# Forgetting attention and channel mix on one core: batch 1's attention weights turned by TensorE, and small operations moved between engines

## The chip, the cores and the metric

One core of a Trainium2 chip runs the whole program. The time is device microseconds from launch to end; the kernel before took 895.82 us, the median of three runs (895.28 to 895.93). PE is TensorE, DVE is VectorE, ACT is ScalarE, POOL is GpSimd and SP the engine that issues the DMAs.

## The reference, cut to what matters

The input has 8 batches, 8 heads, 576 tokens and 64 columns a head; the channel mix has 512 columns outside and 1024 inside.

```python
scores = scale * np.matmul(q, k.transpose(0, 1, 3, 2))
cum = np.cumsum(np.maximum(s, 0.0), axis=-1)
bias = -(cum[:, :, :, None] - cum[:, :, None, :])
scores = np.where(causal, -1000000000.0, scores + np.minimum(bias, 0.0))
scores = scores - np.max(scores, axis=-1, keepdims=True)
attn = np.exp(scores)
attn = attn / (np.sum(attn, axis=-1, keepdims=True) + 1e-09)
x = np.matmul(attn, v)                    # then heads side by side: (8, 576, 512)
xk = mu_k * x + (1.0 - mu_k) * x_prev     # x_prev: x one token earlier
xr = mu_r * x + (1.0 - mu_r) * x_prev
k = np.maximum(xk @ w_k, 0.0)
out = 1.0 / (1.0 + np.exp(-(xr @ w_r))) * (k * k @ w_v)
```

## The kernel before

Attention goes by visits: a visit is two heads of one batch. Batch 0 has eight shorter visits (query tiles 0 to 2 of four head pairs, then tiles 3 and 4), batches 1 to 7 have four visits each over all queries. A head's 576 queries are five tiles of rows: 64 and four times 128. Operands of the big products are split into a high and a low part, so that two or three passes of PE give float32 accuracy.

Batch 0 goes through `scores`. A product lands in a PSUM bank (tags "s" and "t", two banks each). DVE's masking pass (L859) writes the tile to SBUF (W) and gives the row's extreme, ACT takes the exponentials there and the rows' sums (L877), POOL adds a small constant to the sums (L914), DVE inverts them, and POOL scales the rows (L893). Then `weighted` turns the blocks by PE (L1164) and ACT copies them out of PSUM (L1191).

Batches 1 to 7 go through `split_scores`. The tile stays in its PSUM bank: DVE's masking pass writes back there (L945), ACT takes the exponentials in place (L960), POOL prepares the sums (L969), DVE inverts (L976), and `halves` writes two float16 parts of the scaled weights to SBUF, the first by ACT (L985), the second by DVE (L991). The first 64 and the last 128 queries share a bank ("the corner"): for these a DVE operation joins two minima (L1023) and two POOL operations add and copy sums (L1033, L1043). `turn_by_dma` then turns the parts by transposing DMAs into T (four a head), and `sum_values` multiplies them by V's two parts.

V is scaled by POOL (L710) to use float16's range and split by ACT (L715) and POOL (L717). K's high part is a cast on ACT (L777), its low part a difference on POOL (L781), its other copy a cast on POOL (L787); Q's are L792 and L796.

The channel mix goes by 18 chunks of 256 tokens, each of which needs all heads of its tokens. One chunk is 96 products with w_k (L1380), 24 with w_r (L1422) and 48 with w_v (L1447).

Nothing runs in the order of the code. Every instruction is recorded as a task with a cost and a due time, and `Plan` lays them out with a model of the engines; each engine then runs its list in that order, waiting where an operand or a buffer is not there. So the cost written beside an operation (the numbers at the end of `pool(...)` or `act(...)`) sets only the order.

## Time and profile before

| | |
|---|---|
| median of 3 runs | 895.82 us |
| the profiled execution | 894.85 us, its span 893.0 us |
| busy: PE, DVE, ACT, POOL | 831.0, 657.1, 671.5, 453.3 us |
| mean granted clock of PE | 0.96 of full speed |
| PE matmuls | 5094 |

The span is the time from the first to the last instruction of the profiled execution. PE's busy time is not PE at its peak, since matmuls are pipelined and their ends are modelled. In the page's 40 slices PE's granted clock is 0.9 or more in all but five, which lie among the sixth to the eleventh slice, about 112 to 246 us.

### The profile page before, as it was taken

To read this page: it belongs to the slowest core of one execution; us is meant where nothing else is said; L and a number is where in the kernel's file an instruction comes from. 1 tells how busy PE (TensorE), PEld (TensorE's weight loads), DVE (VectorE), ACT (ScalarE), POOL (GpSimd) and SP (SyncE) were. 2 spreads that over 40 slices of the span, in tenths; PEclk is the share of its full clock that TensorE was granted. 3 is DMA by queue.
4 is the path that set the end of the run, shared out by engine and by line. 5 is a ranking of instruction groups with operands and counts; after the bars stand their busy time and mean duration, and the time that the engine had idled before them with its cause. 6 is when DMAs were issued, how large, how long until landed. Compare 5 with 4: busy or idle time off the path is not lost. (4 is left out here: it accounts for less than half of the span.)

```text
span 893.0 us, 16962 instructions
## 1 busy us (share of the span) xinstructions
PE 831.0 (93%) x5094; PEld 664.0 (74%) x5094; DVE 657.1 (74%) x1879; ACT 671.5 (75%) x1703; POOL 453.3 (51%) x755
## 2 busy tenths in 40 slices
PE   9989968866899998999999999999999999999998
PEld 7778747643668777777777877777777778788986
DVE  8989867656788788777887787878787778555431
ACT  6999887656888788788887786878797887545331
POOL 6898884556365555556465465465556552000000
PEclk9999978975799999999999999999999999999999
DMA  8776385687679977796677868679787756401100
GB/s 244 238 230 195 94 182 130 146 160 164 140 161 188 164 169 157 168 187 144 150 182 163 186 156 173 134 153 185 159 163 163 178 102 129 97 22 36 49 25 23
DMA packets 248828, 131.48 MB, mean 147 GB/s; under 512 B 208864, under 2 KB 222176, under 8 KB 248736
## 3 DMA queue, kind: packets, MB, share of 16 engines
q1 hardware_dynamic: 248736, 130.40, 65.0%
q8 instruction: 40, 0.66, 0.3%
q14 instruction: 52, 0.43, 0.2%
HBM read 61.47 MB, written 19.33 MB: 90 GB/s over the span
## 5 line engine op out<-in xcount | busy, mean ns | idle before, releaser
L1380 PE MATMUL m<-xh,w_k 128*128 128x256 f32 x976 | 199.5, 292 | 11.7 <-DVE kl L1409 9.0
L1447 PE MATMUL m<-w_v,kh 128*128 128x512 f32 x528 | 176.8, 400 | 2.5 <-ACT g L1434 2.4
L1380 PEld LDWEIGHTS m<-xh,w_k 128*128 128x128 f32 x976 | 160.7, 194 | 22.6 <-DVE kl L1409 12.2
L1380 PE MATMUL m<-xl,w_k 128*128 128x256 f32 x488 | 140.4, 288 | 0.0
L1447 PEld LDWEIGHTS m<-w_v,kh 128*128 128x128 f32 x528 | 99.0, 189 | 25.7 <-ACT g L1434 2.8
L1447 PE MATMUL m<-w_v,kl 128*128 128x512 f32 x264 | 105.8, 401 | 0.0
L991 DVE SCALAR_TENSOR_TENSOR W<-s,rinv,W 128x64 f16<-128x64 f32 (+2 forms) x168 | 76.6, 458 | 31.8 <-ACT W L985 31.0
L781 POOL TENSOR_TENSOR KH<-raw,KH 64x576 fp32r<-64x576 f32 x64 | 90.7, 1417 | 15.6 <-ACT KH L777 12.1
L1319 ACT ACTIVATE xp<-x,mu 128x256 f32<-128x256 f32 (+3 forms) x184 | 78.3, 426 | 24.8 <-DMA x<-x_d 12.6
L969 POOL TENSOR_SCALAR rinv<-sums 128x1 f32<-128x1 f32 (+1 forms) x224 | 43.1, 192 | 106.2 <-ACT s L960 61.0
L1380 PEld LDWEIGHTS m<-xl,w_k 128*128 128x128 f32 x488 | 94.5, 194 | 2.4 <-issue 0.9
L1422 PE MATMUL m<-w_r,xh 128*128 128x512 f32 x264 | 93.1, 404 | 2.6 <-DVE kl L1409 2.6
L933 PE MATMUL s<-KH,G 128*64 128x64 f32 (+2 forms) x224 | 66.5, 305 | 29.6 <-DVE W L991 29.1
L1326 DVE SCALAR_TENSOR_TENSOR xp<-x,mu,xp 128x256 f32<-128x256 f32 (+3 forms) x184 | 76.5, 416 | 21.1 <-ACT xp L1319 18.3
L796 POOL TENSOR_TENSOR QL<-raw,G 64x576 fp32r<-64x576 f32 (+1 forms) x64 | 85.4, 1334 | 11.6 <-ACT G L792 8.9
L1103 PE MATMUL po<-T,V 128*64 128x512 f16 (+5 forms) x672 | 88.8, 351 | 0.8 <-DMA T<-W 0.8
L985 ACT ACTIVATE W<-s,rinv 128x64 f16<-128x64 f32 (+2 forms) x168 | 76.3, 458 | 16.7 <-DVE rinv L976 7.2
L960 ACT ACTIVATE s<-s,nm 128x64 f32<-128x64 f32 (+2 forms) x168 | 71.4, 425 | 18.6 <-DVE nm L945 14.8
L991 DVE SCALAR_TENSOR_TENSOR W<-t,rinv,W 128x320 f16<-128x320 f32 (+1 forms) x112 | 71.9, 645 | 10.8 <-ACT W L985 10.6
L960 ACT ACTIVATE t<-t,nm 128x320 f32<-128x320 f32 (+1 forms) x112 | 65.0, 581 | 18.7 <-DVE nm L1023 13.7
L933 PEld LDWEIGHTS s<-KH,G 128*128 128x128 f32 (+1 forms) x224 | 41.2, 184 | 50.9 <-DVE W L991 40.7
L945 DVE CUSTOM_DVE_ANT_0 t<-t,lower 128x320 f32<-128x320 f32 (+1 forms) x112 | 66.9, 599 | 10.1 <-PE t L933 9.5
(185 smaller groups left out, 2039.9 us busy)
## 6 DMA issues: line engine op xcount, KB each, us to landing
raw<-in_q SPq DMA_DIRECT2D x112, 144.0 KB
vn<-in_v SPq DMA_DIRECT2D x28, 384.0 KB
raw<-in_k SPq DMA_DIRECT2D x32, 288.0 KB
out<-g SPq DMA_DIRECT2D x36, 256.0 KB
x_d<-xT SPq DMA_DIRECT2D x28, 288.5 KB
x<-x_d SPq DMA_DIRECT2D x11, 514.0 KB
w_k<-in_moe_w_k SPq DMA_DIRECT2D x8, 512.0 KB
w_v<-in_moe_w_v SPq DMA_DIRECT2D x8, 512.0 KB
```

Of the source, the lines that this page charges most:

```text
L781: lambda own=own, other=other, K=K: nc.gpsimd.tensor_tensor(out=K.get()[other], in0=k.get()[own], in1=f32(K.get()[own]), op=ALU.subtract),
L796: lambda x=x, QQ=QQ, QL=QL: nc.gpsimd.tensor_tensor(out=QL.get()[0:64, 0:nq], in0=x.get()[0:64], in1=f32(QQ.get()[0:64]), op=ALU.subtract,),
L933: lambda x=x, G=G, K=K, r=r: nc.tensor.matmul(ps.get()[:m, :n], G.get()[:r, q : q + m], K.get()[:r, k0 : k0 + n], start=x == 0, stop=x == 1,),
L960: lambda: nc.scalar.activation(ps.get()[:, :n], ps.get()[:, :n], AF.Exp, bias=nm.get()[:, i : i + 1], scale=-1.0, accum_out=sums.get()[:, ...
L985: lambda: nc.scalar.activation(part(0), ps.get()[:, :n], AF.Copy, scale=rinv.get()[:, i : i + 1]),
L991: lambda: nc.vector.scalar_tensor_tensor(out=part(1), in0=ps.get()[:, :n], scalar=rinv.get()[:, i : i + 1], in1=part(0), op0=ALU.mult, op1 ...
L1103: nc.tensor.matmul(po.get()[64 * j : 64 * j + 64, start:n], V.get()[:, x, kb, j], at(y, kb, j), start=i == 0, stop=False, tile_position=(0 ...
L1319: lambda z=z: nc.scalar.activation(to(*z), source(1, *z), AF.Copy, scale=mu.ap[:, which, c + z[0] : c + z[0] + 1]),
L1326: lambda z=z: nc.vector.scalar_tensor_tensor(out=to(*z), in0=source(0, *z), scalar=mu1.ap[:, which, c + z[0] : c + z[0] + 1], in1=to(*z), ...
L1380: lambda u=u, f=f, c=c, n=n, w=w, x=x: nc.tensor.matmul(ps.get()[:, u * CT : (u + 1) * CT], weight["k", c, f // 4].get()[:, w, f % 4 * P : ...
L1422: lambda c=c, n=n, x=x, w=w: nc.tensor.matmul(ps.get(), x.get()[:, c, ts], weight["r", c, 0].get()[:, w], start=c == 0 and n == 0, stop=c ...
L1447: lambda f=f, n=n, x=x, w=w: nc.tensor.matmul(ps.get(), x.get()[:, f, ts], weight["v", f, 0].get()[:, w], start=f == 0 and n == 0, stop=f ...
```

## The change

Batch 1 leaves `split_scores` and `turn_by_dma`. It goes through `scores` as batch 0 does, with the sums scaled for float16, and `turn_by_pe` turns the blocks: 14 transposes a head into "t" banks, each block copied by ACT to T as the high float16 part, and the rest written by DVE as the low part, in the layout that `sum_values` reads. Three memsets a head on POOL clear what no block fills. V of batch 1 is laid out after the first head's turn.

For batches 2 to 7 the corner minimum is a DVE reduction, with ACT copying the lower rows; the corner sums and the sums' preparation move from POOL to ACT; K's high part moves from ACT to POOL. V's scaling has a second operation (times 1.0) in all batches. A column of zeros and ones (`upper_rows`) is made once.

```diff
             lambda: nc.gpsimd.tensor_scalar(
-                out=whole(), in0=whole(), scalar1=scales.get()[:, 1:2], scalar2=None, op0=ALU.mult,
+                out=whole(), in0=whole(), scalar1=scales.get()[:, 1:2], scalar2=1.0,
+                op0=ALU.mult, op1=ALU.mult,
             ),
...
+            if b < BY_DMA:
+                act(
+                    lambda own=own, K=K: nc.scalar.copy(K.get()[own], k.get()[own]),
...
+            else:
+                pool(
+                    lambda own=own, K=K: nc.gpsimd.tensor_copy(K.get()[own], k.get()[own]),
+                    [(k, j)], [(K, j)], nk, 150, 0.8333, (2 * j, 2 * j),
+                )
...
         def inverses(i, e, o):
-            pool(
-                lambda: nc.gpsimd.tensor_scalar(
-                    out=rinv.get()[:, i:e], in0=sums.get()[:, o : o + e - i],
-                    scalar1=1.0e-9, scalar2=1.0 / HALF, op0=ALU.add, op1=ALU.mult,
-                ),
...
+            act(
+                lambda: nc.scalar.activation(
+                    rinv.get()[:, i:e], sums.get()[:, o : o + e - i], AF.Copy,
+                    bias=1.0e-9 / HALF, scale=1.0 / HALF,
+                ),
...
             dve(
-                lambda: nc.vector.tensor_scalar(
-                    out=upper(nm, LAST, c + 1), in0=upper(nm, LAST, c + 1),
-                    scalar1=upper(nm, LAST, c), scalar2=upper(nm, c, c + 1),
-                    op0=ALU.min, op1=ALU.min,
-                ),
...
+                lambda: nc.vector.tensor_reduce(
+                    out=upper(nm, LAST + 2, c + 3),
+                    in_=upper(nm, LAST, c + 1).unsqueeze(1).broadcast_to([64, 2, 2]),
+                    axis=mybir.AxisListType.X, op=ALU.min,
+                ),
...
+            act(
+                lambda: nc.scalar.copy(nm.get()[0:64, LAST + 2 : c + 3], nm.get()[0:64, LAST : c + 1]),
...
+            for x, y in ((LAST, c), (c, LAST)):
+                act(
+                    lambda x=x, y=y: nc.scalar.activation(
+                        sums.get()[:, x + 2 : x + 3], sums.get()[:, y : y + 1], AF.Identity,
+                        scale=upper_rows.ap, bias=sums.get()[:, x : x + 1],
+                    ),
...
+    def turn_by_pe(pt):
+
+        T, n = sbuf([P, ROWS * (S - 64)], "T", TURNED, F16), S - 64
...
+            pool(
+                lambda rows=rows, w=w, a=a, step=step: nc.gpsimd.memset(
+                    blocks(w, a, step).bitcast(F32)[rows], 0.0
+                ),
...
+        def turn(ps, place, t, k0, m):
+            pe(
+                lambda: nc.tensor.transpose(
+                    ps.get()[0:m, place : place + P], pt[t].get()[:, k0 : k0 + m], ident.ap
+                ),
...
+        def halves(src, first, second, ps, n, keys, to=0):
+            act(lambda: nc.scalar.copy(first(), src()), [ps], [(T, (0, x)) for x in keys], n)
+            dve(
+                lambda: nc.vector.tensor_tensor(
+                    out=second(), in0=src(), in1=first(), op=ALU.subtract
+                ),
...
+        for kb in range(LAST - 1):
+            ps = bank(1, "t", 2)
+            block(ps, 0, kb)
+        block(ps, 2 * P, LAST - 1)
...
-            Ts.append(turn_by_dma(pt[0]))
+            Ts.append(turn_by_dma(pt[0]) if by_dma(n) else turn_by_pe(pt))
...
-            if n >= PLAIN:
+            if by_dma(n):
                 pt = split_scores(QKs[n][j], parts16[j], None if j else Vs[n][1])
```

POOL's list in batch 1, before: from one scaling of V (vn) to the inverse sums of the next head's tiles (rinv; KL, KH and QL are K's and Q's parts).

```order
L710 TENSOR_SCALAR vn_93<-vn_93,scales_1492 128x768
L694 TENSOR_SCALAR scales_1255<-scales_1255 128x1
L787 CAST KL_533<-raw_284 64x576
L1033 TENSOR_TENSOR sums_135<-sums_135 64x2
L781 TENSOR_TENSOR KH_529<-raw_284,KH_529 64x576
L1043 COPY sums_135<-sums_135 64x2
L717 TENSOR_TENSOR V_1536<-vn_93,V_1536 128x768
L969 TENSOR_SCALAR rinv_239<-sums_135 128x2
```

The same engine in batch 1 of the changed kernel, again from a scaling of V.

```order
L716 TENSOR_SCALAR vn_94<-vn_94,scales_1835 128x768
L809 TENSOR_TENSOR QL_131<-raw_372,G_708 64x576
L724 TENSOR_TENSOR V_1869<-vn_94,V_1869 128x768
L927 TENSOR_SCALAR rinv_250<-sums_136 128x5
L809 TENSOR_TENSOR QL_110<-raw_451,G_425 64x576
L906 TENSOR_SCALAR W_184<-W_184,rinv_250 128x192
L906 TENSOR_SCALAR W_184<-W_184,rinv_250 128x320
L906 TENSOR_SCALAR W_184<-W_184,rinv_250 128x448
L906 TENSOR_SCALAR W_184<-W_184,rinv_250 64x64
L906 TENSOR_SCALAR W_184<-W_184,rinv_250 128x576
L800 CAST KL_549<-raw_92 64x576
```

The corner's two operations and the single inverse sums are gone from POOL; one inverse sum of five columns stands for a whole head, and five scalings of the rows of W follow it.

ACT's list at a corner in batch 2, before: the exponentials of the bank "t" and of the corner's bank "s" (sums_135), and the first halves of the same head (W_1310).

```order
L960 ACTIVATE t_275,sums_135<-t_275,nm_184 128x512
L960 ACTIVATE s_149,sums_135<-s_149,nm_184 128x64
L960 ACTIVATE t_272,sums_157<-t_272,nm_226 128x320
L715 CAST V_1536<-vn_93 128x768
L1319 ACTIVATE xp_297<-x_155,mu 128x192 x2
L960 ACTIVATE s_151,sums_135<-s_151,nm_184 128x192
L985 ACTIVATE W_1310<-s_149,rinv_239 128x64
```

The same engine at a corner in the changed kernel (sums_136, W_2245).

```order
L1046 COPY nm_185<-nm_185 64x2
L999 ACTIVATE W_2420<-s_153,rinv_305 128x448
L974 ACTIVATE t_321,sums_136<-t_321,nm_185 128x512
L974 ACTIVATE s_151,sums_136<-s_151,nm_185 128x64
L1415 ACTIVATE xp_309<-x_157,mu 128x256
L1054 ACTIVATE sums_136<-sums_136,upper_rows 128x1 x2
L1415 ACTIVATE xp_309<-x_157,mu 128x256
L983 ACTIVATE rinv_250<-sums_136 128x2
L999 ACTIVATE W_2245<-s_151,rinv_250 128x64
```

Four small operations of the corner, which stood on POOL and DVE, now stand between ACT's own, with one operation of other work between the exponentials, the sums and the inverse sums.

## Rows read from the trace of the kernel before

**Rows 1.** Busy time by stretch: us, then each engine; clock, DMA share.
```profile
0.00:112.00 112.00, 105.26 (x650) 87.26 (x651) 98.40 (x256) 98.53 (x269) 93.33 (x153) 0.98 0.68 199
112.00:212.00 100.00, 77.85 (x412) 55.88 (x410) 65.64 (x203) 69.51 (x179) 58.63 (x98) 0.79 0.73 157
...
250.00:800.00 550.00, 529.54 (x3352) 421.24 (x3352) 426.61 (x1268) 441.60 (x1119) 281.05 (x473) 1.00 0.73 155
```

**Rows 2.** Timeline of ACT: start, us, engine, line, operation.
```profile
111.83 0.37 ACT L1261 COPY xT<-po 64x256 f32<-64x256 f32 x1
...
212.12 0.69 ACT L1149 ACTIVATE xT<-po,scales 128x512 f32<-128x512 f32 x1
```

**Rows 3.** Busy time by stretch, two slices of 10 us in batch 1.
```profile
190.00:200.00 10.00, 4.11 (x13) 3.00 (x13) 6.21 (x22) 6.78 (x18) 5.98 (x12) 0.50 0.56 118
...
220.00:230.00 10.00, 5.25 (x18) 2.76 (x19) 6.48 (x22) 8.79 (x25) 8.10 (x12) 0.50 0.95 190
```

**Rows 4.** Waits, 112 to 212 us: total us, times, longest.
```profile
PE s L933 <- DVE W L991: 11.7, 6, 5.6
```

**Rows 5.** Timeline of all engines, 193.8 to 201.7 us; idle time before in brackets.
```profile
193.92 2.23 POOL L710 TENSOR_SCALAR vn<-vn,scales 128x768 f32<-128x768 f32 x1
...
196.18 0.83 ACT L715 CAST V<-vn 128x768 f16<-128x768 f32 x1 [1.88 <-POOL vn L710]
...
199.31 0.19 POOL L1033 TENSOR_TENSOR sums<-sums 64x2 f32<-64x2 f32 x1 [0.58 <-ACT s L960]
...
201.54 0.53 PE L933 MATMUL s<-KH,G 128*128 128x192 f32 x1 [5.63 <-DVE W L991]
```

**Rows 6.** Groups by line, POOL: count, busy us, mean ns, idle before.
```profile
L710 POOL TENSOR_SCALAR vn<-vn,scales 128x768 f32<-128x768 f32 x28 | 62.3, 2224 | 6.2 <-DVE scales L692 3.5 <-POOL KH L781 0.9 <-DVE rinv L976 0.2
...
L969 POOL TENSOR_SCALAR rinv<-sums 128x1 f32<-128x1 f32 (+1 forms) x224 | 43.1, 192 | 106.2 <-ACT s L960 61.0 <-ACT t L960 29.6 <-PE s L933 1.5
...
L787 POOL CAST KL<-raw 64x576 fp32r<-64x576 f32 x64 | 42.2, 660 | 42.2 <-PE s L933 31.9 <-issue 6.4 <-PE t L933 1.3
...
L1043 POOL COPY sums<-sums 64x2 f32<-64x2 f32 x56 | 10.0, 178 | 2.2
...
L455 POOL MEMSET T<- 64x64 f32 x4 | 0.6, 238 | 0.1
```

**Rows 7.** Single lines: count, shortest/median/longest ns, first and last start, forms.
```profile
L893 POOL TENSOR_SCALAR W<-W,rinv x40: 311/534/757, 11.2 to 103.8; 128x192 f32<-128x192 f32 x8, 128x320 f32<-128x320 f32 x8, 64x64 f32<-64x64 f32 x8, 128x448 f32<-128x448 f32 x8
...
L877 ACT ACTIVATE W<-W,nm x40: 333/561/788, 7.4 to 98.2; 64x64 f32<-64x64 f32 x8, 128x192 f32<-128x192 f32 x8, 128x320 f32<-128x320 f32 x8, 128x448 f32<-128x448 f32 x8
L877 ACT ACTIVATION_READ_ACCUMULATOR W<-W,nm x40: 184/190/248, 7.6 to 98.9; 128x1 f32 x32, 64x1 f32 x8
...
L1164 PE MATMUL t<-ident,W x112: 270/273/421, 12.5 to 108.3; 128*128 128x128 f32 x80, 128*64 128x128 f32 x32
```

**Rows 8.** Groups by line, ACT and DVE.
```profile
L985 ACT ACTIVATE W<-s,rinv 128x64 f16<-128x64 f32 (+2 forms) x168 | 76.3, 458 | 16.7 <-DVE rinv L976 7.2 <-issue 4.9 <-ACT W L985 1.4
...
L960 ACT ACTIVATE s<-s,nm 128x64 f32<-128x64 f32 (+2 forms) x168 | 71.4, 425 | 18.6 <-DVE nm L945 14.8 <-DVE rinv L976 2.2 <-DVE scales L687 0.3
L985 ACT ACTIVATE W<-t,rinv 128x320 f16<-128x320 f32 (+1 forms) x112 | 67.6, 611 | 3.4 <-ACT t L960 1.5 <-DVE rinv L976 0.5 <-ACT V L715 0.4
...
L960 ACT ACTIVATE t<-t,nm 128x320 f32<-128x320 f32 (+1 forms) x112 | 65.0, 581 | 18.7 <-DVE nm L1023 13.7 <-DVE nm L945 4.3
...
L777 ACT CAST KH<-raw 64x576 fp32r<-64x576 f32 x64 | 42.9, 670 | 2.4 <-PE s L933 1.6
...
L1023 DVE TENSOR_SCALAR nm<-nm 64x2 f32<-64x2 f32 x56 | 28.8, 514 | 2.0
...
L1191 ACT COPY T<-t 128x256 f32<-128x256 f32 (+2 forms) x40 | 14.5, 375 | 2.1 <-PE t L1164 1.9
```

**Rows 9.** Timeline of PE, 12 to 13 us: four transposes in a row.
```profile
12.52 0.60 PE L1164 MATMUL t<-ident,W 128*64 128x128 f32 x4
```

**Rows 10.** Waits, 250 to 800 us: total us, times, longest.
```profile
POOL sums L1033 <- ACT s L960: 53.9, 28, 4.9
```

More of the change, by code (lines that the diff above doesn't have):

```diff
@@ L434, in forgetting_attention_then_channel_mix @@
     HALF = 2.0**15
+    upper_rows = fixed(const.tile([P, 1], F32, name="upper_rows"))
+    for i in range(2):
+        pool(
+            lambda i=i: nc.gpsimd.memset(upper_rows.ap[64 * i : 64 * i + 64], 1.0 * i),
+            [], [(upper_rows, i)], 1, 100,
+        )
     LAST = NQ - 1
@@ L1027, in last_and_first @@
                 ),
[L1028 removed]
+                [(nm, LAST), (nm, c)], [(nm, "u")], 4, quarters=(2, 2),
             )
[L1030 to L1041 removed]
@@ L1074, in turn_by_dma, with parts, blocks, block @@
             )
-        return T
+        def parts(y, kb):
+            return [(T, t) for t in range(max(kb, 1), NQ)]
+        return T, parts
+    def turn_by_pe(pt):
+        T, n = sbuf([P, ROWS * (S - 64)], "T", TURNED, F16), S - 64
+        def blocks(w, a, step, k=LAST - 1):
+            x = T.get().rearrange("p (x q) -> p x q", q=w)
+            return x[:, a : a + step * (k - 1) + 1 : step]
+        for rows, w, a, step, key in (
+            (slice(64, P), 64, 9, 10, 0),
+            (slice(0, 64), 64, 24, 18, 1),
+            (slice(64, P), P, 12, 9, 2),
+        ):
+            pool(
+                lambda rows=rows, w=w, a=a, step=step: nc.gpsimd.memset(
+                    blocks(w, a, step).bitcast(F32)[rows], 0.0
+                ),
+                [], [(T, ("z", key))], w * 3 // 2, 150,
+            )
+        def turn(ps, place, t, k0, m):
[3 more added lines that the diff above has]
+                ),
+                [(pt[t], i) for i in range(3)] + [ident], [ps], P, m, 2 / 2.4,
+            )
+        def halves(src, first, second, ps, n, keys, to=0):
[4 more added lines that the diff above has]
+                ),
+                [ps] + [(T, (0, x)) for x in keys], [(T, (1, x)) for x in keys], n,
+                quarters=(0, to),
+            )
+        def block(ps, place, kb):
+            k = LAST - kb
+            for t in range(kb + 1, NQ):
+                turn(ps, place + P * (t - kb - 1), t, kb * P, P)
+            halves(
+                lambda: ps.get()[:, place : place + P * k].rearrange("p (x q) -> p x q", q=P),
+                lambda: blocks(P, n // P * kb + kb, 1, k),
+                lambda: blocks(P, 9 * kb + 8, 5, k),
+                ps, P * k, [kb],
+            )
+        ps = bank(1, "t", 2)
+        for t in range(1, NQ):
+            turn(ps, P * (t - 1), t, t * P, 64)
+        halves(
+            lambda ps=ps: ps.get()[0:64].rearrange("p (x q) -> p x q", q=64)[:, 0:8:7],
+            lambda: blocks(64, 8 * MIXED + 6, 1, 2)[0:64],
+            lambda: blocks(64, 8 * MIXED + 6, 1, 2)[64:P],
+            ps, P, ["m"], 2,
+        )
+        halves(
+            lambda ps=ps: ps.get()[0:64].rearrange("p (x q) -> p x q", q=64)[:, 1:6:2],
+            lambda: blocks(64, 9, 10)[0:64],
+            lambda: blocks(64, 25, 18)[0:64],
+            ps, 192, ["c"],
+        )
+        for kb in range(LAST - 1):
+            ps = bank(1, "t", 2)
+            block(ps, 0, kb)
+        block(ps, 2 * P, LAST - 1)
+        def parts(y, kb):
+            if kb == LAST:
+                return [(T, (y, "m")) for y in range(2)]
+            found = [(T, (y, kb))]
+            if kb:
+                found += [(T, (y, "c"))] + [(T, ("z", x)) for x in ((1, 2) if y else (0,))]
+            return found
+        return T, parts
@@ L1083, in at @@
         def at(y, kb, j):
-            x = Ts[j].get()
+            x = Ts[j][0].get()
             if not y:
@@ L1110, in both @@
                     )
-            ts = range(max(kb, 1), NQ)
             before = [(po, ("sum", 0))] if i else []
             pe(
-                both, [(V, x)] + [(T, t) for T in Ts for t in ts] + before,
+                both, [(V, x)] + Ts[0][1](y, kb) + Ts[1][1](y, kb) + before,
                 [(po, ("sum", i))] + ([po] if not i else []), n - start, 64, 1.05 / 2.4,
@@ L1143, in sum_values @@
             after = [(po, ("sum", len(todo) + x))] + ([po] if x else [])
-            pe(ends, [(V, x)] + [(T, LAST) for T in Ts] + before, after, 64, 64, 1.05 / 2.4, k)
-            pe(firsts, [(V, x)] + [(T, LAST) for T in Ts], [rest], 64, 64, 1.05 / 2.4, k)
+            pe(ends, [(V, x)] + Ts[0][1](0, LAST) + Ts[1][1](0, LAST) + before, after, 64, 64, 1.05 / 2.4, k)
+            pe(firsts, [(V, x)] + Ts[0][1](0, LAST) + Ts[1][1](0, LAST), [rest], 64, 64, 1.05 / 2.4, k)
         for q0, w, ps in ((0, 64, rest), (64, n, po)):
```

56 lines of the change are left out of this document (26 added, 30 removed).

## The prediction

> **What bounds the kernel now.** I read the busy time by stretch first [rows 1]. The kernel has three different stretches, and the change bears on two of them. Up to 112 us batch 0 is prepared and the weights are turned into two float32 parts: ACT is busy 98.53 of 112 us (0.88) and POOL 93.33 (0.83). From 250 to 800 us PE is busy 529.54 of 550 us (0.96) at the full clock, so that stretch is PE's, with 20.5 us idle. In between, from 112 to 212 us, nothing is full: PE has 77.85 us of work at a mean granted clock of 0.79, ACT 69.51, DVE 65.64, POOL 58.63.
>
> Why nothing is full there is read from the ends of the visits [rows 2]. The last copy of batch 0 into xT starts at 111.83 us and the last one of batch 1 at 212.12 us, so batch 1's four visits (eight heads) take 100.3 us. A chunk of the channel mix has 256 tokens and a batch 576: two chunks lie in batch 0, the third needs batch 1. So PE has two chunks to put between batch 1's heads and then only attention. In the two slices shown [rows 3] PE is busy 4.11 and 5.25 of 10 us, at a clock of 0.50, which is the 1.2 GHz level. It got there after idling. What PE waits for is named next [rows 4]: the matmul of the scores (L933) waits 11.7 us in this stretch for DVE's second half of the weights (L991), that is, for its PSUM bank. Under `split_scores` a bank holds a tile from the product until both halves of the weights are written, and there are two banks of each tag.
>
> One such wait shows the chain [rows 5]. POOL scales V in one operation of 2.23 us from 193.92; ACT's V cast behind it waits 1.88 us, the exponentials wait behind that cast, POOL's sums follow at 199.31, the bank is free only when all that is over, and PE starts again at 201.54 after 5.63 us idle. So the stretch is bound by a chain over four engines with a bank held all along.
>
> What the stretch saves reaches the end: after it PE is 0.96 busy until 800 us [rows 1], and what follows is channel mix alone. PE's work itself shrinks nowhere.
>
> **Batch 1 turned by PE (eight heads).** The products go through `scores`: DVE moves a tile into SBUF in its one masking pass and the bank is free. The chain that held the bank is gone; what is late next is whichever engine has most to do.
> POOL, per head, from its rows [rows 6]. Gone: four inverse sums, 43.1 us over 56 heads, 0.77; the two small corner operations, 2 x 0.18 = 0.36; V's scaling in the new form. The new form is the two-operation tensor_scalar of L893 [rows 7]: 0.757 us for its longest tile, of 576 columns, and 0.311 for the shortest, of 64, so 0.92 for 768 against 2.224, per head half of it, 0.65. Together 1.78. Added: five normalisations of 0.534, 2.67; one inverse sum 0.19; three small memsets of T and one of a column, 0.15 each by L455's 0.6 us for four, 0.5. Together 3.36. Net +1.58, times eight +12.6: 58.6 becomes 71.2 us.
> ACT, per head [rows 7, 8]. Gone: L960, (71.4 + 65.0)/56 = 2.44, and L985, (76.3 + 67.6)/56 = 2.57. Added: five exponentials on SBUF at 0.561, 2.81, and six copies of together 1600 columns at L1191's rate (14.5 us for eight heads of 1280 columns in batch 0), 2.27. The five sum readouts are there before and after. Net +0.07: ACT stays at 70 us.
> DVE loses three of four reciprocals and the corner minimum, and gets six subtractions over 1600 columns for five multiply-subtractions over 1536; I cost this at nothing, hidden by POOL, which has more to do than DVE's 65.64.
> PE gets 14 transposes a head. Four in a row take 0.60 us [rows 9]; less the 0.27 of a single one [rows 7], which the other three follow into the array, that is 0.11 each: 112 are 12.3 us at the full clock. PE's 77.85 us at 0.79 are 61.5 at the full clock, so 73.8 in all.
> SP loses the 32 transposing DMAs of batch 1, so its queue and the loads behind them only get earlier; I take nothing for it.
>
> How long is the stretch then? No engine runs at 1.0. Batch 0 takes the same path, and there POOL reached 0.83 and ACT 0.88 [rows 1]. POOL: 71.2/0.83 = 86 us. ACT: 70/0.88 = 80 us. PE at the full clock 74, at 0.79 93 us. The ends are 80 and 93; I take POOL's 86, because it is the longest of those that the likeliest clock leaves. The gain is 100.3 - 86 = 14.3 us.
>
> The GPSIMD Engine Reference of the Trainium skill (section 4.1, Engine selection) has one-input operations on GpSimd at about line rate. L710's 2.224 us for 768 columns is not that, while L893's 0.757 for 576 is near it. By the page alone the second operation would bring nothing: POOL would be left with 76.4 us and the stretch with 92, a gain of 8 instead of 14.
>
> **Batches 2 to 7 (48 heads).** V's scaling: 1.3 us a visit off POOL; by [rows 5] it was ahead of the sums. The corner minimum: 0.514 us [rows 8] falls to that of another small DVE operation, at best 0.3 saved a head. Both lie beside PE, which is 0.96 busy. POOL no longer stands waiting for ACT's sums (53.9 us before L1033 alone, [rows 10]), so K's and Q's parts behind those waits get earlier. K's high parts cost POOL 0.66 each (as the cast L787, [rows 6]), 48 x 0.66 = 32 us, against 48 x 1.78 = 85 us taken off: hidden in a POOL that is half idle.
> ACT is the other side. It loses 0.67 (L777, [rows 8]) and gets seven small operations a head: the lower rows' minimum, two corner sums, four inverse sums. No such operation is in the trace. From below: 0.19, the readout of one column; from above: 0.333, the shortest exponential, of 64 columns [rows 7]. I take 0.25, nearer to the 64-column one less its columns. Seven are 1.75, less 0.67 is 1.08 a head, 52 us over 48 heads: ACT goes from 441.6 to 493 of 550 us, from 0.80 to 0.90. That is still under PE's 0.96. A small operation that waits for ACT's own sum holds up what is queued behind it on ACT: other heads' halves, and the casts that channel mix waits for. Against the shorter chain I take -2 us for this stretch, between -10 (half of PE's 20.5 idle) and the slower rival below.
>
> **The sum.** 894.85 - 14.3 - 2 = 878.5 us for the profiled execution, which stood 0.97 below the median of the runs; I predict 878.
>
> **Rivals.**
> *The clock stays low.* If PE is granted 0.79 as now, its own work in the stretch, 73.8 at the full clock, takes 93 us, and PE is the bound: gain 7, time 887. For it: PE idles between attention pieces now and the clock is at half [rows 3]. Against it: with the banks free PE's work comes denser, and in batch 0, with the same transposes, the clock is 0.98 [rows 1]. [...]
> *More is gained.* POOL's order lets it run as full as ACT in batch 0 (0.88) and the shorter chain fills half of PE's later idle time: 100.3 - 80 = 20 and 10 more, time 865. For it: POOL waits for ACT only once a head then. Against it: PE's last 3 to 4% are small gaps at many lines.
> *Slower: ACT becomes the bound of batches 2 to 7.* With seven operations at 0.333 it gets 2.33 - 0.67 = 1.66 a head, 80 us: 522 of 550. If each of six of them also waits 0.19 for the sum's readout ahead of it, 55 us more, 577: more than the stretch has, and the stretch grows by 27 against 14 won: 908. It decides from ACT's 564 us on (550 and the 14 won). For it: ACT is in order and each corner sum needs two results of ACT itself. Against it: the order puts other work between (a halves operation or the mixes of the channel mix), and ACT reached 0.88 beside PE in batch 0.
> *No change.* PE's idle time only moves to the wait for batch 2's heads behind 212 us: within 2 us of now, 895.
>
> **Chances.** The forecast (80 to 93 us for the stretch, 872 to 887) 0.56; low clock 0.20; more gained 0.14; slower 0.07; no change 0.03. The forecast, the low clock and the larger gain are all faster: 0.90 by over 0.2% (1.8 us, about what a measurement of this kernel can tell from no change), 0.03 within, 0.07 slower. The range 862 to 892 takes in the forecast's, the low clock's and most of the larger gain and leaves out the slower case.
>
> **What would show it.** Right: batch 1's last xT copy at about 198 us; no wait of over 3 us of the scores' matmul for a PSUM bank before it; V's scaling at 0.9 us; POOL above 0.8 and the clock above 0.9 in the stretch; ACT about 0.9 busy from there to 800. Wrong: that copy at 207 us or later with a clock near 0.8 (the second case); ACT at 0.95 and PE waiting for ACT's casts in batches 2 to 7 (the slower case); V's scaling still above 2 us, which takes 6 us off the gain.

## The result and the profile after

The changed kernel takes 851.41 us (median of 4 runs, 850.28 to 854.97), the kernel before 895.67 beside it (895.28 to 895.93): a ratio of 0.951, with a 95% interval of 0.948 to 0.954. That is 44 us less, where 18 were forecast, and below the range's lower end. The profiled execution took 850.28 us with a span of 848.5; the other stood at 894.85 and 893.0.

The marks that answer to [rows 2], in the timeline of ACT after: the last copy of batch 0, the last of batch 1, and the last visit's.

```profile
105.64 0.37 ACT L1357 COPY xT<-po 64x256 f32<-64x256 f32 x1
...
189.91 0.69 ACT L1245 ACTIVATE xT<-po,scales 128x512 f32<-128x512 f32 x1 [0.68 <-PE po L1218]
...
734.60 0.69 ACT L1245 ACTIVATE xT<-po,scales 128x512 f32<-128x512 f32 x1 [0.82 <-PE po L1218]
```

The ends of these copies cut the span into four stretches. Busy time by stretch, first the kernel after (the answer to [rows 1]; columns as there), then the kernel before with the same cuts.

```profile
0.00:106.00 106.00, 100.54 (x624) 84.50 (x625) 90.94 (x238) 95.59 (x263) 88.33 (x152) 0.97 0.62 197
106.00:190.60 84.60, 82.63 (x555) 63.30 (x553) 60.65 (x203) 66.73 (x190) 70.08 (x120) 1.00 0.37 106
...
190.60:735.30 544.70, 528.89 (x3396) 425.05 (x3396) 434.68 (x1348) 476.23 (x1468) 250.89 (x279) 0.97 0.78 167
735.30:848.50 113.20, 109.46 (x644) 95.85 (x642) 47.74 (x83) 41.60 (x81) 0.00 (x0) 1.00 0.10 32
```

```profile
112.20:212.80 100.60, 78.45 (x413) 56.53 (x412) 65.44 (x203) 70.03 (x180) 58.91 (x101) 0.78 0.73 157
212.80:779.90 567.10, 537.71 (x3391) 424.30 (x3391) 445.08 (x1338) 460.89 (x1176) 300.86 (x503) 0.98 0.75 158
779.90:893.00 113.10, 109.35 (x644) 95.73 (x642) 47.95 (x83) 41.81 (x82) 0.00 (x0) 1.00 0.10 33
```

| stretch | before | after | gain | forecast gain |
|---|---|---|---|---|
| batch 0 | 112.2 | 106.0 | 6.2 | 0 |
| batch 1 | 100.6 | 84.6 | 16.0 | 14.3 |
| batches 2 to 7 | 567.1 | 544.7 | 22.4 | 2 |
| after the last visit | 113.1 | 113.2 | -0.1 | 0 |

So the step on which most of the argument was spent came out, and half of the gain lies where nearly none was expected. Between the two ends of batches 2 to 7 PE has the same matmuls (3391 and 3396 records, 2046 of the channel mix in both), yet its busy time is 8.8 us shorter and its idle time goes from 29.4 to 15.8. The waits that got shorter there are seen in this pair, of batches 2 to 7 alone, before and after (us in total, times, longest): PE for an "s" bank that DVE frees, ACT's cast of V for POOL's scaling, and ACT for the corner minimum. The second has no row in the answer after any more.

```profile
PE s L933 <- DVE W L991: 17.3, 17, 4.1
...
ACT V L715 <- POOL vn L710: 11.6, 15, 1.8
...
ACT t L960 <- DVE nm L1023: 10.1, 18, 2.0
```

```profile
PE s L947 <- DVE W L1005: 6.9, 10, 1.6
...
ACT t L974 <- DVE nm L1038: 1.9, 5, 0.6
```

### The profile page after: what moved, and what is told of

Read it like the earlier page. It is cut to its first block, busy times and chain, and to the rows that moved or that the text cites. A ratio compares the mean times of both kernels' runs of the same rounds, so it can differ in the third digit from the quotient of the medians.

```text
span 848.5 us, 17084 instructions
## 1 busy us (share of the span) xinstructions
PE 821.5 (97%) x5214; PEld 668.7 (79%) x5214; DVE 634.0 (75%) x1871; ACT 680.1 (80%) x1999; POOL 409.3 (48%) x549
## 4 chain that ended last, share of the span: by engine, by line
PE 83%; DVE 7%; ACT 7%; issue 2%; DMA 2%; SPq 0%; POOL 0%; ACTq 0%; DVEq 0%; POOLq 0%
PE m L1543 22%; PE m L1476 15%; PE m L1518 10%; PE po L1200 8%; PE s L947 5%; PE t L947 4%; PE po L1346 2%; PE s L857 2%; PE t L1543 2%; PE t L1476 2%; PE s L1476 2%; PE t L1116 2%; PE t L1260 1%; PE s L846 1%; PE s L835 1%
## 5 line engine op out<-in xcount | busy, mean ns | idle before, releaser
L1415 ACT ACTIVATE xp<-x,mu 128x256 f32<-128x256 f32 (+3 forms) x184 | 78.7, 428 | 22.4 <-DMA x<-x_d 13.4
L790 POOL CAST KH<-raw 64x576 fp32r<-64x576 f32 x48 | 31.7, 660 | 119.2 <-PE s L947 106.0
L1200 PE MATMUL po<-T,V 128*64 128x512 f16 (+5 forms) x672 | 79.7, 339 | 1.0 <-DMA T<-W 1.0
L1005 DVE SCALAR_TENSOR_TENSOR W<-s,rinv,W 128x192 f16<-128x192 f32 (+2 forms) x144 | 65.3, 456 | 12.1 <-ACT W L999 9.8
L999 ACT ACTIVATE W<-s,rinv 128x192 f16<-128x192 f32 (+2 forms) x144 | 66.2, 463 | 4.0 <-DVE rinv L990 3.1
L1005 DVE SCALAR_TENSOR_TENSOR W<-t,rinv,W 128x320 f16<-128x320 f32 (+1 forms) x96 | 61.8, 645 | 10.1 <-ACT W L999 9.5
L974 ACT ACTIVATE s<-s,nm 128x64 f32<-128x64 f32 (+2 forms) x144 | 62.1, 431 | 8.2 <-DVE nm L959 7.4
L959 DVE CUSTOM_DVE_ANT_0 t<-t,lower 128x320 f32<-128x320 f32 (+1 forms) x96 | 57.5, 601 | 11.3 <-PE t L947 10.4
L999 ACT ACTIVATE W<-t,rinv 128x320 f16<-128x320 f32 (+1 forms) x96 | 58.7, 618 | 2.0 <-DVE rinv L990 1.8
L947 PE MATMUL s<-KH,G 128*128 128x192 f32 (+2 forms) x192 | 52.8, 289 | 7.1 <-DVE W L1005 6.9
L1518 PEld LDWEIGHTS m<-w_r,xh 128*128 128x128 f32 x264 | 49.2, 189 | 12.0 <-DVE kl L1505 0.9
```

Source lines behind the costliest of these rows:

```text
L947: lambda x=x, G=G, K=K, r=r: nc.tensor.matmul(ps.get()[:m, :n], G.get()[:r, q : q + m], K.get()[:r, k0 : k0 + n], start=x == 0, stop=x == 1,),
L974: lambda: nc.scalar.activation(ps.get()[:, :n], ps.get()[:, :n], AF.Exp, bias=nm.get()[:, i + o : i + o + 1], scale=-1.0, accum_out=sums.g ...
L999: lambda: nc.scalar.activation(part(0), ps.get()[:, :n], AF.Copy, scale=rinv.get()[:, i : i + 1]),
L1005: lambda: nc.vector.scalar_tensor_tensor(out=part(1), in0=ps.get()[:, :n], scalar=rinv.get()[:, i : i + 1], in1=part(0), op0=ALU.mult, op1 ...
L1200: nc.tensor.matmul(po.get()[64 * j : 64 * j + 64, start:n], V.get()[:, x, kb, j], at(y, kb, j), start=i == 0, stop=False, tile_position=(0 ...
L1415: lambda z=z: nc.scalar.activation(to(*z), source(1, *z), AF.Copy, scale=mu.ap[:, which, c + z[0] : c + z[0] + 1]),
```

## The experiments

Times are medians; the ratio is to the kernel before, on the same chip, with its 95% interval. "Stretches" are batch 0, batch 1, batches 2 to 7 and the rest, in us, cut here at the starts of the last copies, which puts them up to 0.7 us off a cut at the ends.

### The parts of the change, each alone

The first question was which part the 22 us of batches 2 to 7 belong to: the theory was V's scaling, rivals the corner or a mere reordering of the list.

**Turn alone (turn_only).** The kernel after, with the other edits undone.

> The kernel before with batch 1 turned by PE and nothing else of the change. Theory A (each edit pays in its own batches; the 22 us that batches 2 to 7 lost come from the edits to their small operations): batch 1's stretch is 16 us shorter and batches 2 to 7 keep their 567 us, so 874 to 880 us. Rival B (once batch 1 is dense, batches 2 to 7 run denser too, whatever their small operations): 850 to 862, with batches 2 to 7 at about 545 us.

**All but the turn (no_turn).** The same number decides who casts K's high part, so batch 1's casts go to POOL as well.

```diff
-    BY_DMA = 2
+    BY_DMA = 1
```

> The changed kernel, but batch 1 goes by split_scores and transposing DMAs like batches 2 to 7, with all other edits. Theory A: batches 2 to 7 take about 545 us, batch 1's stretch 100 us less its share of the same edits (22/6 = 4 us): 866 to 873 us. Rival B: close to before, 888 to 895.

**V's second operation alone (v_only).** On the kernel before:

```diff
-scalar2=None, op0=ALU.mult,
+scalar2=1.0, op0=ALU.mult, op1=ALU.mult,
```

> The kernel before with V's scaling in two operations alone: POOL gets 1.3 us a visit back. Theory A1 (the inverse sums on POOL were the chain, and V's scaling stood ahead of them): 8 to 12 us faster, 884 to 888. Rival A2 (what counts is that ACT needs no other engine for the sums): 0 to 3 us faster, 893 to 896.

**The corner alone (corner_only).** On the kernel before, the reduction on DVE, and all sums on ACT, as in the change's diff.

> The kernel before with the corner minimum as a DVE reduction and all sums on ACT, in batches 1 to 7; V's scaling in one operation, K's high part on ACT. ACT gets seven small operations a head more, 1.8 us. Theory A2: 15 to 20 us faster, 876 to 881, in batches 2 to 7 above all. Theory A1: 4 to 8 us faster, 888 to 892, since V's scaling still holds POOL and ACT. Rival C (ACT has too much without moving K's part): slower than before.

**A cost number alone (order_only), and K's high part (k_only).** Only the written cost of one cast, which the change also alters; then K's part on POOL from batch 2 on, with the same number.

```diff
-                [(k, j)], [(KB, 0)], nk, 244, 0.8333, (2 * j, 0),
+                [(k, j)], [(KB, 0)], nk, 150, 0.8333, (2 * j, 0),
```

> The kernel before with one number of the change alone, the cost written beside K's third copy on POOL (244 becomes 150), which sets the order of the lists and no instruction. Theory A: within 0.5% of before, 890 to 899, so that the gains of 15 us of single edits are theirs. Rival O (any new order is worth about 15 us against the one of before): 875 to 885.

> The kernel before with K's high part cast by POOL in batches 2 to 7 and no other edit (with the cost 150 of that copy's neighbour). ACT loses 0.67 us a head, POOL gets 0.66. Theory A (POOL's waits for the sums hold K's parts and the next head): 0 to 8 us slower, 895 to 903. Rival D (ACT's time is what counts in these batches): 8 to 15 us faster, 880 to 887.

**K's high part back on ACT (after_k_act)**, in the kernel after, with the 244 of its neighbour; and **half of batch 1 turned by PE (turn_half)**, its first two visits, the last two by DMA as the batches behind it, a test of whether the change of path between batch 1 and batch 2 costs something:

```diff
-        return visits[n][0] >= BY_DMA
+        return n >= PLAIN + NP // 2
```

> The changed kernel with K's high part back on ACT (and the cost 244 of its neighbour). ACT has seven more operations a head and keeps the cast. Theory D2 (the small operations on ACT pay only together with K's part off ACT, since ACT was at 505 of 566 us with the first alone): 8 to 15 us slower than the changed kernel, 859 to 866. Rival: the same as the changed kernel, 850 to 855.

> The changed kernel with the first two visits of batch 1 turned by PE and the last two by transposing DMAs, all other edits kept. Theory H (the hole at the change from one path to the other, 27 us at a clock of 0.62 behind batch 1, is the price of the turn: with no turn at all the first visit of batch 2 took 19.8 us): the change of path falls where chunks of batch 0 are left for PE, so 843 to 848. Rival: between the changed kernel and the one without a turn, 852 to 858.

| kernel | us | ratio | stretches |
|---|---|---|---|
| before | 895.67 | | 111.8, 100.3, 567.1, 113.8 |
| turn_only | 879.06 | 0.983 (0.979 to 0.987) | 105.9, 82.1, 573.1, 114.1 |
| v_only | 879.24 | 0.984 (0.980 to 0.987) | 111.0, 94.1, 557.4, 113.9 |
| corner_only | 876.37 | 0.982 (0.977 to 0.986) | 110.8, 92.4, 566.0, 105.0 |
| k_only | 893.71 | 0.999 (0.997 to 1.001) | 112.1, 97.3, 567.5, 114.2 |
| order_only | 897.29 | 1.003 (1.000 to 1.005) | 112.9, 103.1, 567.7, 114.0 |
| no_turn | 858.62 | 0.960 (0.957 to 0.963) | 114.2, 94.5, 535.4, 113.1 |
| turn_half | 859.51 | 0.961 (0.959 to 0.964) | 107.9, 99.5, 533.5, 115.7 |
| after | 851.41 | 0.951 (0.948 to 0.954) | 105.6, 84.3, 544.7, 113.9 |
| after_k_act | 849.35 | 0.951 (0.947 to 0.955) | 106.1, 85.6, 540.0, 116.0 |

What follows. Everything but the turn gives 37.1 us, and that is nearly the sum of its parts alone (V 16.4, corner 19.3, K 2.0: 37.7). K's move is worth nothing that can be told, in either direction. The turn alone gives 16.6, but on top of the rest only 7. In this set batches 2 to 7 get much shorter only where V's edit and the corner's stand together (534 to 545 us); alone they leave 557 and 566. But a list also moves pieces of the channel mix from one stretch to another, so a length means little without the work in it: PE has 3378 to 3396 matmuls in this stretch in all these runs but corner_only, which has 3459 there and 70 fewer behind the last visit. The hypothesis about the change of path fell: with the change inside batch 1 the first visit of batch 2 is short, 20.5 us, as in no_turn (19.8; 27.8 before, 27.7 after), but batch 1 takes 99.5, and the total is no_turn's.

Of the expectations, turn_only's and order_only's came. corner_only's total came, but not its place: it has 7.9 us in batch 1 and 8.8 behind the last visit, and hardly any in batches 2 to 7. v_only came 5 us and no_turn 7 us below what was expected, turn_half 12 above, k_only between its two ranges, and after_k_act just below its rival's.

Busy time by stretch of turn_only (batch 1, batches 2 to 7) and of no_turn (the same), columns as above:

```profile
106.30:188.70 82.40, 80.91 (x547) 61.51 (x545) 59.22 (x202) 66.82 (x186) 71.97 (x120) 1.00 0.36 104
188.70:761.80 573.10, 538.18 (x3395) 430.01 (x3396) 450.73 (x1348) 463.54 (x1184) 308.67 (x517) 0.96 0.75 159
```

```profile
114.50:209.40 94.90, 76.73 (x431) 56.32 (x431) 66.44 (x215) 75.48 (x239) 49.37 (x58) 0.80 0.78 174
209.40:744.70 535.30, 523.14 (x3394) 420.99 (x3394) 428.85 (x1331) 473.04 (x1450) 245.92 (x268) 0.98 0.79 167
```

In this pair the turn is what brings the full clock into batch 1 (1.00 against 0.80); under another list it does not (0.82 in turn_costs_true, below). The other edits empty POOL (308.67 to 245.92 us), and what follows is shorter with them.

### The list, with no instruction changed

v_only saves 16 us with 28 operations that are 1.3 us shorter: 37 us in all on POOL, which is half idle. A rival came up that the first set could not exclude: the list of before had been laid out with a wrong number. V's scaling is written as 768 x 0.8333 + 210 ns, 0.85 us, and takes 2.22 [rows 6]; after the edit it takes 0.91, close to what had been written all along. The corner minimum is written as 0.14 us and takes 0.51 on average [rows 8]. So I changed only these numbers; the instructions stay what they were.

**V's number (v_true_cost).**

```diff
-            [(scales, 1)], [vn], n, 210,
+            [(scales, 1)], [vn], n, 1584,
```

> The kernel before with one number changed, the cost written beside V's scaling on POOL: 768 columns x 0.8333 + 210 = 0.85 us becomes 2.22 us, what the operation takes. No instruction changes. Theory M (the gain of 15 us from the two-operation form came from the list: it was laid out for 0.85 us, and what stands right behind V's scaling waited 1.4 us on all engines each time): most of it, 8 to 15 us, comes back, 881 to 888. Rival T (the 1.3 us of POOL's time are in the chain however the list lies): 892 to 898.

**The corner minimum's number (min_true_cost), and both (costs_true).**

```diff
-                [], [(nm, LAST), (nm, c)], 2, extra=140, quarters=(2, 2),
+                [], [(nm, LAST), (nm, c)], 2, extra=512, quarters=(2, 2),
```

> The kernel before with one number changed, the written cost of the corner minimum on DVE: 0.14 us becomes 0.51. No instruction changes. Theory M (the list's wrong durations): 8 to 12 us faster as the new form was, 884 to 888. Rival T2 (here the 0.36 us of DVE's time count): 893 to 898.

> The kernel before with both numbers changed, V's scaling 2.22 us and the corner minimum 0.51 us. No instruction changes. Theory M: the two gains add for the most part, 868 to 875. Rival: one list is as good as the other once one number is right, 875 to 880.

**Halves of the corner edit (min_only, sums_only):** the reduction alone, and the sums on ACT alone, on the kernel before.

> The kernel before with the corner minimum alone in its new form (DVE reduction, ACT copies the lower rows), in batches 1 to 7; the sums stay on POOL. The old form takes 0.51 us on DVE, and its written cost is 0.14; the new one takes 0.15, plus 0.19 on ACT beside it. Theory: 0.36 us a head of the chain, 56 heads; at V's rate (15.5 us for 28 times 1.3 us) 8 us: 886 to 890. Rival S (the gain of 17 us is that of the sums): 893 to 897.

> The kernel before with the corner sums and the preparation of all sums on ACT alone, in batches 1 to 7; the minimum in its old form. Theory: 9 us faster, 885 to 889, the other half of the 17 us. Rival S: 15 us or more faster, 876 to 881. Rival: nothing, 893 to 897, since ACT takes 0.39 us for each of two corner sums where POOL took 0.19.

| kernel | us | ratio | stretches |
|---|---|---|---|
| v_true_cost | 877.14 | 0.980 (0.978 to 0.982) | 112.3, 85.3, 567.9, 109.9 |
| min_true_cost | 870.72 | 0.971 (0.966 to 0.976) | 112.9, 81.3, 567.5, 105.1 |
| costs_true | 867.53 | 0.968 (0.963 to 0.973) | 110.8, 86.8, 559.2, 110.0 |
| min_only | 883.56 | 0.987 (0.985 to 0.989) | 116.9, 88.4, 562.8, 114.0 |
| sums_only | 884.09 | 0.988 (0.986 to 0.989) | 115.0, 90.1, 564.1, 113.0 |

V's right number alone saves as much as its faster form, 18.5 us against 16.4, with the operation still at 2.2 us, as its row in v_true_cost says (count; shortest, median, longest ns):

```profile
L710 POOL TENSOR_SCALAR vn<-vn,scales x28: 2210/2228/2231, 100.9 to 738.3; 128x768 f32<-128x768 f32 x28
```

The right number of the corner minimum saves 25 us, more than the whole corner edit (19.3), and both together 28. Part of where it comes from is seen in the waits, whole run: of before, of v_true_cost, then of costs_true.

```profile
PE s L933 <- DVE W L991: 29.1, 23, 5.6
...
ACT t L960 <- DVE nm L1023: 13.7, 22, 2.0
ACT V L715 <- POOL vn L710: 13.5, 16, 1.9
...
PE t L933 <- DVE W L991: 1.6, 2, 1.0
```

```profile
ACT t L960 <- DVE nm L1023: 21.7, 31, 2.7
...
PE s L933 <- DVE W L991: 13.5, 13, 4.0
...
ACT V L715 <- POOL vn L710: 3.9, 4, 1.6
```

```profile
ACT t L960 <- DVE nm L1023: 8.8, 15, 1.2
...
PE t L933 <- DVE W L991: 8.4, 6, 4.8
...
PE s L933 <- DVE W L991: 3.2, 4, 1.6
```

Told that the scaling takes long, the list no longer lets ACT's cast wait for it as long: that wait falls from 13.5 to 3.9 us, while the one for the corner minimum rises to 21.7. Told the second number too, the wait for the corner minimum falls to 8.8, and PE's wait for a bank (both tags) goes from 30.7 us, with 1.6 for "t", to 11.6. No instruction became faster.

The direction is as expected, the sizes are not: v_true_cost came 4 us, min_only 2 and min_true_cost 13 us below their ranges, sums_only and costs_true within 1 us of theirs. In min_true_cost these waits fall by little (9.1 us for the corner minimum, 24.7 for a bank), and 22 of its 26 us in the profiled span are PE's busy time (831.0 to 809.0) with the same instructions. About half of that is in batch 1 (78.45 to 66.61 us for 413 and 408 matmuls, at a granted clock of 0.78 and 0.90). How one number, off by 0.37 us, does that is open.

### The changed kernel with right numbers

**Right costs of the small new operations (after_true_costs).** As measured in the kernel after: ACT's corner minimum copy, corner sums and inverse sums, and DVE's reduction (the changed ends of the lines).

```diff
-1, 92,
+1, 205,
...
-[(nm, LAST), (nm, c)], [(nm, "u")], 4, quarters=(2, 2),
+[(nm, LAST), (nm, c)], [(nm, "u")], 4, extra=149, quarters=(2, 2),
...
-[(nm, LAST), (nm, c)], [(nm, "l")], 2, 92,
+[(nm, LAST), (nm, c)], [(nm, "l")], 2, 190,
...
-[(sums, x + 2)], 1, 92,
+[(sums, x + 2)], 1, 387,
```

> The changed kernel with the written costs of its small operations set to what its trace shows (ACT's corner sums 0.09 to 0.39 us, the sums' preparation 0.09 to 0.21, the lower rows' copy 0.09 to 0.19; DVE's corner reduction 0.07 to 0.15). No instruction changes. Theory M: 4 to 10 us faster than the changed kernel, 841 to 847. Rival T: within 3 us of it, 848 to 854.

**V in one operation again, with its right number (after_v_one_true)**, in the kernel after: `scalar2=None`, and 1584 for 210.

> The changed kernel with V's scaling in one operation of 2.22 us and that cost written beside it. Theory M: as the changed kernel, 849 to 855, since POOL is under half busy there. Rival T: 859 to 866.

**The turn with the right numbers: on the old corner and V (turn_costs_true), and taken out of after_true_costs (no_turn_true).**

> The kernel before with batch 1 turned by PE and both numbers right; V's scaling in one operation, the old minimum, sums on POOL, K's cast on ACT. Theory M: the faster forms of V's scaling and of the minimum bring nothing of their own, only the sums on ACT are missing against the changed kernel: 855 to 864. Rival T (the operations' time counts): 868 or more.

> The changed kernel with the true written costs of its small operations (as in after_true_costs) and without the turn by PE in batch 1. Theory M2 (the turn is worth what batch 1's stretch gains, 10 to 15 us, whatever the list): 852 to 860 against 845 with the turn. Rival L (once the list's durations are right the turn brings nothing, as against costs_true, where it cost 14 us): 838 to 848.

**A number that should not matter (after_244):** the cast's cost, 150 back to 244, in the kernel after.

> The changed kernel with the written cost of K's third copy back at 244 (it takes 0.66 us; 150 gives 0.63, 244 gives 0.72), no instruction changed. It shows how far a list can move the time where no duration gets better: theory, within 0.5% of the changed kernel, 847 to 856; rival (any other list moves the time by 10 us): outside of 843 to 860.

| kernel | us | ratio | stretches |
|---|---|---|---|
| after_true_costs | 845.07 | 0.944 (0.942 to 0.946) | 118.7, 65.5, 545.2, 114.1 |
| after_v_one_true | 847.07 | 0.945 (0.939 to 0.950) | 109.4, 82.8, 539.9, 116.1 |
| no_turn_true | 857.51 | 0.959 (0.954 to 0.963) | 107.1, 78.1, 555.9, 113.9 |
| turn_costs_true | 881.82 | 0.983 (0.978 to 0.988) | 112.8, 83.4, 570.9, 109.8 |
| after_244 | 850.80 | 0.951 (0.947 to 0.955) | 109.5, 91.1, 538.3, 113.4 |

after_v_one_true settles V: with the slow operation and its right number the kernel after is no slower (847.07 against 851.41), as v_true_cost is no slower than v_only. The faster form is worth nothing in itself here; what it did was make a wrong number true. after_244 and order_only are the controls: an arbitrary change of a number, which also reorders the list, moves the total by 0.6 us down and 1.6 up, though it shifts up to 7 us from one stretch to the next. A gain of 18 to 28 is far outside that. But these controls change a number by 0.09 us, the corrections by 0.37 and 1.37, and no run changes another number by as much: how much of the gain any larger shift of the list could bring is not shown.

after_true_costs is the fastest kernel that was run, 6 us under the changed one, the intervals apart. Its stretch of batch 1 and batches 2 to 7:

```profile
119.00:184.90 65.90, 64.59 (x458) 47.91 (x457) 51.24 (x171) 56.47 (x162) 55.70 (x98) 1.00 0.34 100
184.90:730.00 545.10, 532.31 (x3454) 430.59 (x3453) 429.28 (x1351) 481.03 (x1467) 254.38 (x283) 1.00 0.80 169
```

Batch 0 and batch 1 run into each other here: batch 0 ends 13 us later than in the kernel after, batch 1 has 458 matmuls instead of 555 left and ends 6 us earlier. The end of batch 1 is the better mark than either length.

Along one way the 50.6 us of after_true_costs go in steps: 28.1 by the two numbers alone (to 867.53), 10.0 by the corner's operations off POOL and DVE's 0.51, with V and K (to 857.51), and 12.4 by the turn (to 845.07). Along another they are shared out quite differently. With the turn in place the same two numbers bring nothing: turn_costs_true is at 881.82, turn_only at 879.06. And from turn_costs_true to after_v_one_true, which differ by the corner's move and by K's part, worth nothing alone, 34.8 us are won. turn_costs_true came at its rival's range (868 or more), 18 us above the theory's. The expectations of after_true_costs, no_turn_true and after_244 came, and after_v_one_true is 2 us below its theory. So the gains do not add up, and no single share of the 44 us belongs to the numbers, to the corner or to the turn.

What happens in turn_costs_true is seen in its stretches (batch 1, batches 2 to 7):

```profile
113.20:196.90 83.70, 72.38 (x414) 48.69 (x412) 58.27 (x192) 64.59 (x178) 73.24 (x119) 0.82 0.37 96
196.90:767.80 570.90, 559.19 (x3563) 446.01 (x3563) 457.00 (x1348) 465.30 (x1184) 304.87 (x511) 1.00 0.74 160
```

Its batches 2 to 7 are not slower for their work: they hold 168 matmuls more than turn_only's. The loss lies in batch 1, which is as long as turn_only's with 133 matmuls fewer, nearly all of the channel mix (76 for 203), with PE idle for 11.3 us and a clock of 0.82. Why the list leaves PE so little there was not found.

## Why the prediction was right or wrong

**The step that failed** is "Both lie beside PE, which is 0.96 busy", and with it "Against the shorter chain I take -2 us for this stretch". 22.4 us came. Three things were wrong in it.

First, it took the list as given. I read V's 2.224 us in [rows 6] and the corner minimum's 0.514 in [rows 8] and priced the operations' own time. I never held these durations against the numbers written beside them, which stood in the code: 0.85 and 0.14. The list expected the results 1.4 and 0.4 us too early. v_true_cost, min_true_cost and costs_true show what that was worth without the turn: up to 28 us without any faster instruction. In batches 2 to 7 costs_true takes 559.2 us for 114 matmuls of the channel mix more than before. At 0.16 us each, PE's mean there before (537.71/3391), these are 18 us, so that by this estimate the work of before would take it about 541 us, no more than the kernel after's 544.7.

Second, it took the busy share for a bound. Of the 22.4 us 13.6 were idle time of PE, and 8.8 came out of its busy time: the same matmuls went from 537.71 to 528.89 busy us at about the same granted clock (0.98 and 0.97), which suggests that some of the waiting had been counted as work. The page Trainium Kernel Development and Optimization of the Trainium skill (section Performance Expectations) says that matmul busy time is a bad measure of closeness to the limit, since matmuls are pipelined, and names the share of weight loads instead, beside a share of the peak arithmetic. The trace agrees in so far as PEld is 0.75 of that stretch before and 0.78 after (424.30 of 567.10, 425.05 of 544.70), lower than PE's share both times; how much of the rest can be won no run shows.

Third, what the corner's move takes off POOL was called hidden. Without the turn and with right numbers the move is worth 10.0 us together with V and K (costs_true to no_turn_true), with the turn 34.8 (turn_costs_true to after_v_one_true). Its two halves alone give 12.1 (min_only) and 11.6 us (sums_only) on the list of before. Whether POOL's freed time counts in it, DVE's shorter minimum, or that ACT need not wait for POOL's sums, is not separated. So it is open which share of the 22.4 us each of these has in the changed kernel.

The sum itself has a slip: 878.5 is for the profiled execution, and with the 0.97 that it stood below the median it gives 879.5, not 878. Of the rivals "More is gained" comes nearest with 865, but it too allowed these batches only half of PE's 20.5 idle us.

**Batch 1** was right in size, which is in part luck: 84.6 us for 86, but in the other kernels with the whole turn it is 65.5 to 91.1 us long, the latter (after_244) by one number and no change of the total. POOL, taken as the longest, is 70.08 us busy for 71.2, a share of 0.83, just the one taken; ACT 66.73 for 70; the clock 1.00, so the low-clock case fell here. Only PE has more than worked out, 82.63 us for 73.8 (30 more records than before's 413 and the 112 transposes), and is 0.98 busy: whether POOL or PE limits the stretch is not told by shares, and no run separates them. The bank waits of [rows 4] are no longer among the stretch's longest eleven waits, of which the shortest is 1.4 us. Of the two slices of [rows 3] only the first lies in batch 1, which ends at 212 us; the second, 220 to 230, is in batch 2's first visit, and what it shows the turn does not mend. Busy time of two slices after, columns as above: the least busy of PE's eight from 106 to 186 us, for 4.11 us at a clock of 0.50, and the one as far behind batch 1 as the second, 6.68 us at a clock of 0.50 for 5.25 at 0.50.

```profile
176.00:186.00 10.00, 8.50 (x45) 5.84 (x44) 6.90 (x27) 8.80 (x29) 7.64 (x16) 1.00 0.60 159
...
198.00:208.00 10.00, 6.68 (x22) 4.88 (x21) 8.41 (x29) 9.79 (x33) 6.19 (x9) 0.50 0.92 199
```

The cause I gave, banks held along a chain, is only half shown. The list's right numbers alone bring the stretch to 81 to 87 us with the banks held as before (min_true_cost 81.3, v_true_cost 85.3, costs_true 86.8). So shortening the chain and laying it out rightly bring the stretch to nearly the same length, and [rows 5] showed both: the scaling's 2.23 us, and work queued as if it took 0.85. The stretches do not hold the same work, though: PE has 408 to 432 matmuls in these, and 443 besides the 112 transposes in the kernel after.

**PE's transposes.** The 0.11 us apart are confirmed in the timeline of PE after: eight take 1.03 us, (1.03 - 0.27)/7 = 0.109.

```profile
143.96 1.03 PE L1116 MATMUL t<-ident,W 128*64 128x128 f32 x8
```

**V's scaling** came out as taken from L893: 0.908 us for 0.92. The rule that the prediction cites from the GPSIMD Engine Reference of the Trainium skill (section 4.1, Engine selection), one-input operations on GpSimd at about line rate, by which the second operation would bring nothing to POOL, did not hold for the form with one operation: 2.224 us. The row of the kernel after:

```profile
L716 POOL TENSOR_SCALAR vn<-vn,scales x28: 897/908/920, 118.3 to 702.2; 128x768 f32<-128x768 f32 x28
```

**ACT in batches 2 to 7** did not become the bound. Its small operations per head are one copy at 0.190, two sums at 0.389 and four inverse sums at 0.21, 1.81 us for the 1.75 taken, in these groups (count, busy us, mean ns, idle before):

```profile
L1054 ACT ACTIVATE sums<-sums,upper_rows 128x1 f32<-128x1 f32 x96 | 32.0, 389 | 0.1
L790 POOL CAST KH<-raw 64x576 fp32r<-64x576 f32 x48 | 31.7, 660 | 119.2 <-PE s L947 106.0 <-issue 12.2 <-POOL V L724 0.4
L983 ACT ACTIVATE rinv<-sums 128x1 f32<-128x1 f32 x144 | 29.7, 213 | 0.5
...
L1046 ACT COPY nm<-nm 64x2 f32<-64x2 f32 x48 | 9.1, 190 | 11.8 <-DVE nm L959 9.9 <-DVE rinv L990 1.4
```

Yet ACT's busy time rose by 15.3 us (460.89 to 476.23), not by 52. Its records overlap, so durations do not add up on it: the groups of this stretch, each by itself, add up to 547 us before and 605 after, 58 us more, and the sums alone would be 37 us (96 of 389 ns) and count 32. The share is 0.87, near the 0.90 forecast, in part because the stretch got shorter. The waits feared for the sums come to nothing: ACT is idle before its corner sums for 0.1 us and before its inverse sums for 0.5 us in all. K's 32 us on POOL lie hidden, as taken: the cast mostly waits for PE (106.0 us).

**Not foreseen at all** were the 6.2 us of batch 0. Kernels with the turn end it at 105.6 to 118.7 us, those without at 107.1 to 116.9; the lists trade work between it and batch 1. **Of the "no change" rival** nothing came true: 27 us behind batch 1 PE has 19.52 us busy at 0.62 after and 19.48 at 0.60 before, the same hole in both.

```profile
190.60:217.60 27.00, 19.52 (x91) 13.09 (x91) 21.92 (x73) 22.94 (x74) 16.41 (x23) 0.62 0.89 176
```

```profile
212.80:239.80 27.00, 19.48 (x101) 12.91 (x101) 19.73 (x67) 20.19 (x57) 13.24 (x23) 0.60 0.74 146
```

## What to carry to other kernels

Where a program lays out the order from written costs, hold each of them against the trace before anything else: two wrong numbers were worth 28 us of 896 here, and each alone as much as the faster form of its operation or more (18.5 against 16.4 us for V, 25 against 12.1 for the corner minimum). When a faster operation pays more than its own time, ask whether it made such a number true, and test that by correcting the number alone, with an arbitrary change of another number, as large, as the control. Do it in more than one kernel: with the turn in place the same corrections brought nothing. And don't cap a gain at part of an engine's idle time: a stretch with PE 0.95 busy got 4% shorter with the same matmuls, two fifths of it out of PE's busy time.
